# Moving the load of v of chunk 1 from GpSimd's queue to SyncE's, and that of chunk 0 from SyncE's to ScalarE's

## The chip, the cores and the metric

The kernel runs on one core of one Trainium2 chip. The metric is the device time of one execution in microseconds (us). An execution also leaves a profile: the span from the first to the last instruction is some 1.7 to 2.1 us shorter than the time. All times inside an execution are counted from the start of the span.

## The reference

Linear attention with a decay per head, in blocks, followed by a two-layer feed-forward network with an exact GELU:

```python
batch, n_heads, seq, head_dim = (4, 8, 768, 64)      # q, k, v float32; lam: one decay per head
...
intra = np.einsum('bhic,bhjc->bhij', qb, kb) * Dmask[None]
intra = np.einsum('bhij,bhjd->bhid', intra, vb)
inter = np.einsum('bhid,bhde->bhie', qb * lam_pow[None], kv_state)
out[:, :, sl] = intra + inter
...
n_tokens, d_model, d_ff = (3072, 512, 2048)
h = x @ w_in
g = 0.5 * h * (1.0 + erf(h * inv_sqrt2))
return (g @ w_out)
```

## The kernel before

The kernel cuts the attention into 24 chunks of 128 tokens (four batches, six chunks each). A prelude computes the attention of chunks 0 to 3; from then on TensorE (PE) runs the feed-forward matmuls without a break (busy for 191.12 of 191.20 us from 19.0 to 210.2 us), and the attention of later chunks is slipped in between them. Below, this second part is "the dense part"; it begins with the first `h_ps` matmul.

The loads at the start. A load by GpSimd casts float32 to bfloat16 on the way (128 KB a load on the page); v of chunk 0 alone goes by SyncE as float32 (256 KB) and is cast by ScalarE (0.61 us):

```python
def chunk_of(name, n):
    b, so = n % B, n // B
    return dram[name][b, :, so * C:(so + 1) * C, :].rearrange("h si d -> si h d")   # runs of 64 floats

def load(n, name):
    raw[n, name] = qkv_pool.tile([128, H, D], BF16, tag=name, name=f"{name}_t")
    nc.gpsimd.dma_start(raw[n, name], chunk_of(name, n))

load(0, "k")
lam_b = consts.tile([128, H], F32)
nc.sync.dma_start(lam_b, lam[None, :].to_broadcast((128, H)))
v_f = consts.tile([128, H, D], F32)
nc.sync.dma_start(v_f, chunk_of("v", 0))
# ... two iotas
for item in "q0 k1 q1 k2 q2 v1 v2 k3 q3".split():
    load(int(item[1]), item[0])
# ...
load_w_in(0, 4)          # the first of four slices of w_in
load_w_in(4, 8)
load(3, "v")
# ... two more slices of w_in, four of w_out
```

The prelude. `keep_warm(n)` issues n matmuls on zeros, which keep PE busy between pieces of real work:

```python
keep_warm(11)
# ... begin
transposes(live[0], lambda: keep_warm(1, new=False))
keep_warm(2, new=False)
scores(live[0])
late_powers()
nc.scalar.copy(live[0].v, v_f)
keep_warm(2, new=False)
transposes(live[1], lambda: keep_warm(1, new=False))
keep_warm(2)
outputs(live[0])
transposes(live[2], lambda: keep_warm(1, new=False))
nc.scalar.activation(warm, pos, ACT.Gelu)
scores(live[1])
keep_warm(1)
scores(live[2])
keep_warm(2)
outputs(live[1])
keep_warm(2)
outputs(live[2])
transposes(live[3])
keep_warm(3)
scores(live[3])
keep_warm(6)
```

In the dense part GpSimd multiplies k and q of later chunks by their decays, while DVE updates the state of a batch with two products:

```python
# GpSimd, out of first_requests()
for n in (2 * M, 2 * M + 1):
    request(n)                                   # q_hat = q * lam_p
for n in range(M, 2 * M):
    decay_k(live[n], nc.gpsimd)                  # k_dec = k * lam_m
prefetch(2 * M + 3)                              # six loads
for n in (2 * M, 2 * M + 1):
    decay_k(live[n], nc.gpsimd)
# DVE, out of next_state()
nc.vector.tensor_add(tmp, kv_ps, states[c.b])    # one input in PSUM
nc.vector.tensor_mul(new, tmp, lam_blk)          # both inputs in SBUF
```

Of the kernel before, what the change touches and what calls it, by code (L numbers as in the profile page):

```python
# [8 lines left out]
F32 = mybir.dt.float32  # L9
BF16 = mybir.dt.bfloat16  # L10
# [5 lines left out]
def kernel(  # L16
# [10 lines left out]
    nc = tc.nc  # L27

    B, H, S, D = q.shape
# [16 lines left out]
    consts = ctx.enter_context(tc.tile_pool(name="consts", bufs=1))  # L46
    w_pool = ctx.enter_context(tc.tile_pool(name="w", bufs=1))
    qkv_pool = ctx.enter_context(tc.tile_pool(name="qkv", bufs=12))
# [8 lines left out]
    raw = {}  # L57
    dram = dict(q=q, k=k, v=v)

    def chunk_of(name, n):  # L60
        b, so = n % B, n // B
        return dram[name][b, :, so * C:(so + 1) * C, :].rearrange("h si d -> si h d")
# [4 lines that stand above are left out]
# [2 lines left out]
    load(0, "k")  # L69
    lam_b = consts.tile([128, H], F32)  # L70
    nc.sync.dma_start(lam_b, lam[None, :].to_broadcast((128, H)))
    v_f = consts.tile([128, H, D], F32)
    nc.sync.dma_start(v_f, chunk_of("v", 0))

    pos = consts.tile([128, 1], F32)
    row = consts.tile([128, C], F32)
    nc.gpsimd.iota(pos, pattern=[[0, 1]], base=0, channel_multiplier=1, allow_small_or_imprecise_dtypes=True)  # L77
    nc.gpsimd.iota(row, pattern=[[1, C]], base=0, channel_multiplier=0, allow_small_or_imprecise_dtypes=True)  # L78
    for item in "q0 k1 q1 k2 q2 v1 v2 k3 q3".split():
        load(int(item[1]), item[0])  # L80

    w_in_t = w_pool.tile([128, NK1, d_ff], BF16)
# [51 lines left out]
    def late_powers():  # L134
        nc.scalar.activation(lam_c, ln_col, ACT.Exp, scale=float(C))
        nc.scalar.activation(lam_p, ln, ACT.Exp, scale=pos)
# [17 lines left out]
    live = {}  # L154

    def bank(shape, dtype, tag, name):
        return ps.tile(shape, dtype, tag=tag, name=name, bufs=4)
# [13 lines left out]
    def transposes(c, between=lambda: None):  # L171

        t_ps = [bank([128, HP, C], BF16, "m" if c.so == 0 else "sc", "t_ps") for _ in range(2)]
        for dst, src in zip(t_ps, (c.k, c.q)):
            for hp in range(HP):
                nc.tensor.transpose(dst[:, hp, :], src[:, 2 * hp:2 * hp + 2, :], ident)  # L176
            if src is c.k:
                between()
        c.kT = work_pool.tile([128, HP, C], BF16, tag="kT", name="kT")
        c.qT = work_pool.tile([128, HP, C], BF16, tag="qT", name="qT")  # L180
        nc.scalar.copy(c.kT, t_ps[0])
        nc.vector.tensor_mul(c.qT, t_ps[1], lam_q)  # L182
# [37 lines left out]
    def inter(c):  # L220
        c.o_ps = bank([128, HP, C], F32, "sc", "o_ps")
        if c.so > 0:
            for hp in range(HP):
                nc.tensor.matmul(c.o_ps[:, hp, :], states[c.b][:, hp, :], c.qT[:, hp, :],  # L224
                                 start=(hp == 0), stop=False, skip_group_check=True)

    def intra(c):
        for hp in range(HP):
            for hi in range(2):
                nc.tensor.matmul(c.o_ps[hi * D:(hi + 1) * D, hp, :], c.v[:, 2 * hp + hi, :], c.sc_m[:, hp, hi, :],  # L230
                                 start=(c.so == 0 and hp == 0), stop=True, skip_group_check=True)
        x_o = xT[c.so][:, :, c.b * C:(c.b + 1) * C]
        if c.so < 2:
            nc.scalar.copy(x_o, c.o_ps)  # L234
        else:
            nc.vector.tensor_copy(x_o, c.o_ps)  # L236

    def outputs(c):
        inter(c)
        intra(c)  # L240
# [78 lines left out]
    def keep_warm(n, new=True):  # L319

        if new:
            idle_ps[0] = bank([128, 512], F32, "m", "idle_ps")
        for _ in range(n):
            nc.tensor.matmul(idle_ps[0], idle[:, :128], idle, start=True, stop=True)  # L324
# [2 lines left out]
    nc.vector.tensor_mul(dmask, cmask[:, None, :].to_broadcast((128, H, C)),  # L327
                         lam_m[:, :, None].to_broadcast((128, H, C)))
    keep_warm(11)
    raw[0, "v"] = qkv_pool.tile([128, H, D], BF16, tag="v", name="v_t")  # L330
    for n in range(M):
        begin(n)
    transposes(live[0], lambda: keep_warm(1, new=False))
    keep_warm(2, new=False)
    scores(live[0])
    late_powers()
    nc.scalar.copy(live[0].v, v_f)
    keep_warm(2, new=False)
    transposes(live[1], lambda: keep_warm(1, new=False))
    keep_warm(2)  # L340
    outputs(live[0])
    transposes(live[2], lambda: keep_warm(1, new=False))
    nc.scalar.activation(warm, pos, ACT.Gelu)
    scores(live[1])
# [91 lines left out]
    for g in range(1, NG - 1):  # L436
        n = (g + 1) * M
# [45 lines left out]
```

## Time and profile before

| | before |
|---|---|
| time, median of the first 3 runs | 214.99 us (214.94 to 215.33) |
| span of the profiled run | 213.3 us |
| PE busy | 206.8 us, 97% |
| k of chunk 0 landed | 5.4 us |
| first transposes on PE | 5.86 us |
| first w_in slice landed | 18.91 us |
| dense part starts | 18.96 us |

A timeline line reads: start, duration, engine, source line, operation, output<-inputs, count, and in brackets the idle time before it and what ended it. The prediction shows the lines themselves.

### The profile page before, as it was taken

How to read it: one execution, taken by the hardware profiler on the slowest of the kernel's cores; microseconds unless marked ns; L12 is line 12 of the kernel's file. 1: busy time of each engine (PE TensorE's matmuls, PEld its weight loads, DVE VectorE, ACT ScalarE, POOL GpSimd, SP SyncE). 2: the span in 40 equal slices, each digit the busy share in tenths (PEclk: the TensorE clock that was granted, in tenths of full speed). 3: DMA queues.
4: the chain of work that ended last, by engine and by line, in shares of the span. 5: the costliest groups of instructions: out<-in, count | busy, mean ns of one | idle time of the engine just before them, and what ended most of it. 6: DMA issues, size and time to landing. Idle time of an engine off the chain costs nothing.

```text
span 213.3 us, 3586 instructions
## 1 busy us (share of the span) xinstructions
PE 206.8 (97%) x1474; PEld 105.3 (49%) x1474; DVE 77.8 (36%) x122; ACT 87.2 (41%) x153; POOL 103.7 (49%) x117
## 2 busy tenths in 40 slices
PE   7979999999999999999999999999999999999994
PEld 2444754556655445445445445445445445444442
DVE  4758040164395747147327047227042312000000
ACT  5653754325655221464321465321455321566121
POOL 7992433792997966929949297592000000000000
PEclk9999999999999999999999999999999999999999
DMA  8999999999999699999999989999330012100112
GB/s 87 134 160 185 206 208 187 155 213 146 151 112 116 76 124 113 233 134 65 122 110 160 199 102 129 100 168 101 123 74 0 3 49 98 52 0 0 49 49 98
DMA packets 100271, 24.48 MB, mean 115 GB/s; under 512 B 92960, under 2 KB 97312, under 8 KB 100256
## 3 DMA queue, kind: packets, MB, share of 16 engines
q0 software_dynamic: 78064, 13.51, 85.8%
q1 hardware_dynamic: 22192, 10.76, 24.6%
q8 instruction: 11, 0.18, 0.3%
q14 instruction: 4, 0.03, 0.1%
HBM read 27.27 MB, written 6.29 MB: 157 GB/s over the span
## 4 chain that ended last, share of the span: by engine, by line
PE 90%; POOL 4%; DMA 4%; issue 0%; ACT 0%; POOLq 0%
PE h_ps L263 40%; PE o_ps L275 38%; DMA w_in_t<-in_moe_w_in_dram 4%; PE o_ps L230 3%; PE sc_ps L197 3%; PE o_ps L224 2%; PE kv_ps L209 2%; POOL k_t L66 2%; PE o_ps L289 2%; POOL q_t L66 2%; PE t_ps L176 1%; POOL v_t L66 1%; ACT o_sb L293 0%; POOL row L78 0%; POOL pos L77 0%
## 5 line engine op out<-in xcount | busy, mean ns | idle before, releaser
L263 PE MATMUL h_ps<-x_t,w_in_t 128*128 128x512 bf16 (+2 forms) x432 | 86.5, 356 | 0.3 <-DMA w_in_t<-in_moe_w_in_dram 0.3
L275 PE MATMUL o_ps<-w_out_t,g_t 128*128 128x512 bf16 x368 | 82.8, 379 | 0.0
L265 ACT ACTIVATE g_t<-h_ps 128x512 bf16<-128x512 f32 (+1 forms) x99 | 57.8, 584 | 38.9 <-PE h_ps L263 38.7
L263 PEld LDWEIGHTS <-w_in_t 128*128 128x128 bf16 x432 | 39.2, 98 | 41.6 <-DMA w_in_t<-in_moe_w_in_dram 0.8
L275 PEld LDWEIGHTS <-g_t 128*128 128x128 bf16 x368 | 35.0, 98 | 41.2
L201 DVE TENSOR_TENSOR sc_m<-sc_ps,dmask 128x512 bf16<-128x512 f32 x48 | 29.9, 682 | 36.8 <-PE sc_ps L197 36.8
L280 ACT COPY o_sb<-o_ps 128x512 f32<-128x512 f32 x23 | 13.5, 586 | 69.7 <-PE o_ps L275 69.7
L189 POOL TENSOR_TENSOR q_hat<-q_t,lam_p 128x512 bf16<-128x512 bf16 x16 | 17.1, 1071 | 27.8 <-DMA q_t<-in_q_dram 12.5
L66 POOL DMA_DIRECT2D k_t<-in_k_dram x24 | 22.1, 920 | 6.4 <-DMA w_in_t<-in_moe_w_in_dram 3.8
L66 POOL DMA_DIRECT2D q_t<-in_q_dram x24 | 21.7, 903 | 3.4 <-DMA w_out_t<-in_moe_w_out_dram 3.3
L66 POOL DMA_DIRECT2D v_t<-in_v_dram x23 | 21.0, 914 | 3.4 <-DMA w_out_t<-in_moe_w_out_dram 1.7
L216 DVE TENSOR_TENSOR tmp<-kv_ps,state 128x512 f32<-128x512 f32 x16 | 11.0, 685 | 27.8 <-PE kv_ps L209 27.8
L169 POOL TENSOR_TENSOR k_dec<-k_t,lam_m 128x512 bf16<-128x512 bf16 x16 | 18.1, 1161 | 0.0
L217 DVE TENSOR_TENSOR state<-tmp,lam_blk 128x512 bf16<-128x512 f32 x16 | 13.7, 856 | 0.6
L236 DVE CAST x_t<-o_ps 128x512 bf16<-128x512 f32 x16 | 10.2, 680 | 9.4 <-PE o_ps L230 9.4
L324 PE MATMUL idle_ps<-idle 128*128 128x512 bf16 x34 | 11.7, 462 | 1.2 <-DVE idle L105 1.2
L182 DVE TENSOR_TENSOR qT<-t_ps,lam_q 128x512 bf16<-128x512 bf16 x8 | 5.5, 690 | 15.5 <-PE t_ps L176 15.4
L230 PE MATMUL o_ps<-sc_m,v_t 128*64 128x128 bf16 x192 | 8.6, 223 | 0.2
L197 PEld LDWEIGHTS <-kT 64*128 64x128 bf16 x192 | 5.7, 94 | 6.1 <-issue 3.6
L197 PE MATMUL sc_ps<-qT,kT 64*128 64x128 bf16 x192 | 8.0, 217 | 0.7 <-DVE qT L182 0.4
L230 PEld LDWEIGHTS <-v_t 128*64 128x64 bf16 x192 | 5.9, 109 | 3.2 <-issue 1.6
L234 ACT CAST x_t<-o_ps 128x512 bf16<-128x512 f32 x8 | 4.6, 585 | 5.3 <-PE o_ps L230 5.2
(41 smaller groups left out, 71.9 us busy)
## 6 DMA issues: line engine op xcount, KB each, us to landing
out_dram<-o_sb SPq DMA_DIRECT2D x23, 256.0 KB, 2.5
k_t<-in_k_dram POOLq DMA_DIRECT2D x24, 128.0 KB, 5.4
q_t<-in_q_dram POOLq DMA_DIRECT2D x24, 128.0 KB, 6.0
v_t<-in_v_dram POOLq DMA_DIRECT2D x23, 128.0 KB, 6.1
w_in_t<-in_moe_w_in_dram POOLq DMA_DIRECT2D x4, 512.0 KB, 11.1
w_out_t<-in_moe_w_out_dram POOLq DMA_DIRECT2D x4, 512.0 KB, 17.9
v_f<-in_v_dram SPq DMA_DIRECT2D x1, 256.0 KB, 3.6
kT<-k_t SPq DMA_TRANSPOSE x16, 4.0
```

What stands on the lines that cost most here:

```text
L66: nc.gpsimd.dma_start(raw[n, name], chunk_of(name, n))
L169: eng.tensor_mul(c.k_dec, c.k, lam_m[:, :, None].to_broadcast((128, H, D)))
L189: nc.gpsimd.tensor_mul(q_hat, c.q, lam_p[:, :, None].to_broadcast((128, H, D)))
L197: nc.tensor.matmul(sc_ps[hi][:, hp, :], c.kT[p, hp, :], c.qT[p, hp, :], start=True, stop=True)
L201: nc.vector.tensor_mul(c.sc_m[:, :, hi, :], sc_ps[hi], dmask_r[:, :, hi, :])
L217: nc.vector.tensor_mul(new, tmp, lam_blk)
L230: nc.tensor.matmul(c.o_ps[hi * D:(hi + 1) * D, hp, :], c.v[:, 2 * hp + hi, :], c.sc_m[:, hp, hi, :], start=(c.so == 0 and hp == 0), stop=T ...
L263: nc.tensor.matmul(h_ps[:, f, :], w, x_t[:, ki, lo:hi], start=(ki == 0 and f == 0), stop=(ki == NK1 - 1), skip_group_check=True)
L265: nc.scalar.activation(g_t[:, kf:kf + n_kf, lo:hi], h_ps, ACT.Gelu)
L275: nc.tensor.matmul(om[io], g_t[:, kf, io * C:(io + 1) * C], w_out_t[:, kf, :], start=(kf == 0), stop=(kf == NK2 - 1))
L280: nc.scalar.copy(o_sb, om[io])
L324: nc.tensor.matmul(idle_ps[0], idle[:, :128], idle, start=True, stop=True)
```

## The change

The intent: GpSimd issues its loads one after another (most take 0.88 to 0.95 us), and the first w_in slice stands behind ten of them. Taking v of chunk 1 out of that row should bring the weights in earlier. In exchange ScalarE casts one more tile.

```diff
-    v_f = consts.tile([128, H, D], F32)
-    nc.sync.dma_start(v_f, chunk_of("v", 0))
+    v_f = consts.tile([128, 2, H, D], F32)
+    nc.scalar.dma_start(v_f[:, 0], chunk_of("v", 0))
+    nc.sync.dma_start(v_f[:, 1], chunk_of("v", 1))
 ...
-    for item in "q0 k1 q1 k2 q2 v1 v2 k3 q3".split():
+    for item in "q0 k1 q1 k2 q2 v2 k3 q3".split():
 ...
-    nc.scalar.copy(live[0].v, v_f)
+    nc.scalar.copy(live[0].v, v_f[:, 0])
 ...
     outputs(live[0])
+    nc.scalar.copy(live[1].v, v_f[:, 1])
     transposes(live[2], lambda: keep_warm(1, new=False))
```

More of the change, by code (lines that the diff above doesn't have):

```diff
@@ L329 @@
     keep_warm(11)
-    raw[0, "v"] = qkv_pool.tile([128, H, D], BF16, tag="v", name="v_t")
+    for n in range(2):
+        raw[n, "v"] = qkv_pool.tile([128, H, D], BF16, tag="v", name="v_t")
     for n in range(M):
```

## The prediction

The forecast is 214.8 us: 214.99 less 0.33, the mean of its two cases (0 and -0.67 us), plus 0.1 for the maximum of two landings. The 0.27 us by which the software queue falls back rested on the author's estimate, from 290 left-over packets at 1085 per us. The 0.1 and the two halves are guesses.

> **What bounds the kernel now.** I read the page first: engine shares and the chain that ended last.
>
> ```profile
> span 213.3 us, 3586 instructions
> PE 206.8 (97%) x1474; PEld 105.3 (49%) x1474; DVE 77.8 (36%) x122; ACT 87.2 (41%) x153; POOL 103.7 (49%) x117
> PE 90%; POOL 4%; DMA 4%; issue 0%; ACT 0%; POOLq 0%
> ```
>
> TensorE is busy for 97% of the span, and 90% of the last chain is its work. Next, the table of stretches, which splits the span where I expected the regimes to change. Columns: stretch, its length, then busy time and instruction count of PE, PEld, DVE, ACT and POOL, the granted clock, the DMA share, GB/s.
>
> ```profile
> 10.50:11.70 1.20, 0.20 (x3) 0.09 (x3) 0.00 (x0) 1.18 (x3) 1.20 (x3) 1.00 2.29 146
> 11.70:18.70 7.00, 6.55 (x66) 3.13 (x66) 5.16 (x9) 2.64 (x5) 4.97 (x7) 1.00 1.46 173
> 19.00:210.20 191.20, 191.12 (x1352) 98.02 (x1352) 66.27 (x102) 76.62 (x133) 88.17 (x93) 1.00 1.08 113
> ```
>
> From 19.0 to 210.2 us PE is busy for 191.12 of 191.20 us at full clock. The change alters none of that work, so the end moves only as far as the first matmul of the dense part (h_ps) moves. That starts at 18.96 us. What sets it? The chain in order of time, early pieces:
>
> ```profile
> 1.26 1.06 POOL k_t L66
> ...
> 7.09 1.75 POOL v_t L66 x2
> 8.84 0.87 POOL k_t L66
> 9.71 0.79 POOL q_t L66
> 10.50 8.41 DMA w_in_t<-in_moe_w_in_dram
> 18.91 0.05 issue
> 18.96 4.07 PE h_ps L263 x24
> ```
>
> By this chain, GpSimd issues ten chunk loads one after another and then the first w_in slice, which lands 8.41 us later. This is what the change attacks. But the chain shows only the last releaser, so I read PE's own timeline for the second latest:
>
> ```profile
> 10.23 0.38 PE L324 MATMUL idle_ps<-idle 128*128 128x512 bf16 x1
> 11.61 0.40 PE L176 MATMUL t_ps<-ident,q_t 128*128 128x128 bf16 x4 [1.00 <-DMA q_t<-in_q_dram]
> ...
> 16.90 0.40 PE L197 MATMUL sc_ps<-qT,kT 64*128 64x128 bf16 x8
> 17.23 1.47 PE L324 MATMUL idle_ps<-idle 128*128 128x512 bf16 x6
> 18.96 4.07 PE L263 MATMUL h_ps<-x_t,w_in_t 128*128 128x384 bf16 x24 [0.26 <-DMA w_in_t<-in_moe_w_in_dram]
> ```
>
> PE waits for w_in only 0.26 us. Its in-order prelude ends at 18.70, and this prelude is tied to another transfer: the q of chunk 2, which lands at 11.6 and before which PE idles 1.00 us. From there to 18.70 is 7.09 us of transposes, scores, outputs and filler matmuls in a fixed order. So two branches end within 0.2 us: **branch W**, the w_in slice (18.91), and **branch Q**, q of chunk 2 plus 7.09 us (18.70).
>
> Last, the DMA view in narrow windows, packets by queue. The two lines below are for 3.5 to 4.0 us; a chunk load is 1024 packets.
>
> ```profile
> q1 hardware_dynamic: 346, 0.09, 76.7%
> q0 software_dynamic: 178, 0.02, 71.0%
> ```
>
> In 3.0 to 3.5 us the hardware queue alone moved 482; in 4.0 to 4.5 the software queue moved 546. All three are near 500 packets per half microsecond. For 5.0 to 12.5 us the view counts 8134 software packets, that is 542 per half microsecond: from about 3 us on the shared engines are full. One chunk load costs 1024 / 1085 per us = 0.94 us of them, against 0.87 us of issue on GpSimd, so service and not issue sets the pace.
>
> [...]
>
> **The change part by part.**
> - *Removed from the software queue*: v of chunk 1, 0.87 us of issue and 0.94 us of service ahead of w_in. (By my count nine loads stay ahead of the first slice; the tenth, v of chunk 3, is between slices.) It stood **behind** q of chunk 2, so branch W gains up to 0.94 us and branch Q nothing.
> - *Added to the hardware queues*: another 1024 packets early. In before, v of chunk 0 is issued at 1.20 us, sends its first packets near 2.3 and is done by about 4.2. In after, ScalarE can issue v of chunk 0 at 0.7, half a microsecond earlier, with SyncE's load beside it. From the half-microsecond counts I estimate some 900 packets by 3.0 us (v0 run forward half a microsecond about 680, v1 about 220), 500 more by 3.5 and 350 by 4.0, which leaves some 300 of 2048. [...] The software queue falls back by about 290 / 1085 = 0.27 us, and as it is full from there on, it keeps the delay.
> - *Branch W*: -0.94 + 0.27 = -0.67, so 18.24 us.
> - *Branch Q*: +0.27 from the same delay. Against it: lags from issue to landing for k0, q0, k1, q1, k2, q2 are 4.1, 3.7, 4.2, 4.2, 4.2, 5.4 us. Only the last is out of line, and between 9.0 and 9.5 us the packet count dips to 426. If that was a chance stall, q2 would land at 6.18 + 4.2 + 0.27 = 10.65 next time and branch Q would end at 17.74; if it is systematic, at 18.97. I give each half.
> - *ScalarE*: one issue (0.4 us, taken from SyncE's rows) lies before 2.43 us, where ScalarE waits for lam until 3.61: free. The second cast (0.61 us, as the v_t<-v_f row) goes after x_t of chunk 0 at 10.68 us. It pushes kT of chunk 2 from 11.18 to about 11.8, needed at 12.79, and the Gelu table load's end from 12.47 to 13.1, with ScalarE's next work at 14.40: free.
> - *Sum*: start of h_ps is the later branch. Systematic: max(18.24, 18.97) = 18.97, no gain. Chance: max(18.24 + 0.05, 17.74) = 18.29, a gain of 0.67. The mean is -0.33; the maximum of two jittering landings costs some 0.1, so about -0.2 us from 214.99, which is 214.8.
>
> **Rivals.** *Full gain*: the hardware loads are through before GpSimd's first packets (3.4 us), nothing is delayed, W gains 0.94 and Q lands early: 214.0 to 214.1. For it: engines idle until 2.3 us. Against: the first q1 packets come slowly, about 200 per half microsecond before 3.0, and 2048 packets at 500 per half microsecond need 2 us. *Branch Q takes the place of W*: v traffic delays k0 and q2 by more than I think [...], say 0.5 to 0.7, and the prelude with its six filler matmuls ends at 19.2 to 19.4: 215.3 to 215.4. For it: only 0.26 us separates the branches. Against: PE has 1.00 us of idle ahead of q2, so delays of k0 alone are absorbed. *ScalarE becomes the bound*: the cast delays kT of chunk 2 and outputs of chunk 1. It would need over 1 us more than I count; up to +0.3 us. *A late lam*: its 128 tiny packets now compete with v; ln, lam_m, dmask and qT slip by a few tenths, again ahead of the 1.00 us of idle: nothing.
>
> **Range and chances.** Best case -0.9, worst +0.5, both unlikely: 214.2 to 215.4 holds 8 in 10. 2% is 4.3 us. The whole prelude is 19 us and neither branch can move by that; a build whose dense part runs otherwise is all I leave: faster 0.01, same 0.98, slower 0.01.
>
> **What would show it.** The first h_ps start should move from 18.96 to 18.3 to 19.0 and the dense part keep 191.2 us. The w_in slice should be issued near 9.63 instead of 10.50 and land near 18.2. k of chunk 0 should land 0.2 to 0.3 us later than 5.4. If branch Q binds, h_ps shows no wait for w_in and follows the six filler matmuls at once. I am wrong if the dense part changes length, if k of chunk 0 doesn't slip, or if ScalarE shows up as releaser in the prelude.

## The result, and the profile after

The changed kernel took 217.04 us (median of 5 fast runs, 216.72 to 218.15), the kernel before in the same rounds 214.96 us (214.74 to 215.33). A ratio here is the mean time of one kernel's fast runs over that of the other's of the same rounds, so not quite the ratio of the medians: 1.0107, 95% interval 1.0078 to 1.0136. The change made the kernel about 1% slower. By the 2% rule this is "same", and the predicted range (214.2 to 215.4) did not hold it.

From the page of the changed kernel: the span, the engines, the granted PE clock in 40 slices (in tenths of full speed) and the chain that ended last.

```profile
span 215.1 us, 3562 instructions
PE 206.2 (96%) x1449; PEld 106.0 (49%) x1474; DVE 75.8 (35%) x122; ACT 87.8 (41%) x154; POOL 102.7 (48%) x116
...
PEclk9889999999999999999999999999999999999999
...
PE 89%; DVE 5%; DMA 3%; issue 1%; POOL 1%; ACT 0%; POOLq 0%; DVEq 0%
```

New are the two 8s in the clock row, the second and third slices, and DVE with 5% of the chain. (PE shows 25 fewer matmuls, but the weight loads are 1474 as before: some matmul records are missing.)

PE's timeline of the changed kernel, the lines that answer to those of before:

```profile
1.19 4.69 PE L325 MATMUL idle_ps<-idle 128*128 128x512 bf16 x11 [1.19 <-DVE idle L106]
7.47 0.40 PE L177 MATMUL t_ps<-ident,k_t 128*128 128x128 bf16 x4 [1.58 <-DMA k_t<-in_k_dram]
...
13.66 0.39 PE L177 MATMUL t_ps<-ident,q_t 128*128 128x128 bf16 x4
...
19.26 1.47 PE L325 MATMUL idle_ps<-idle 128*128 128x512 bf16 x6
20.57 4.06 PE L264 MATMUL h_ps<-x_t,w_in_t 128*128 128x384 bf16 x24
```

The dense part starts at 20.57 us instead of 18.96. It no longer waits for w_in: the slice was issued at 9.62 and landed 6.8 us later, at 16.4 us, 2.5 us earlier than before, and lay unused for 4 us. Nor does PE wait for q of chunk 2 at 13.66. What is late is the very first input: k of chunk 0 landed 6.2 us after its issue at 1.25, so at 7.45 us instead of 5.4, and PE idled for 1.58 us ahead of it.

The table of stretches for two windows of 3.41 us in the changed kernel. Columns: stretch, length, busy time and count of PE, PEld, DVE, ACT and POOL, granted clock, DMA share, GB/s. The bounds are the moments at which the trace's clock record changes.

```profile
5.58:8.99 3.41, 1.55 (x13) 0.62 (x11) 1.35 (x2) 2.56 (x9) 3.41 (x5) 1.00 2.43 155
8.99:12.40 3.41, 3.06 (x21) 1.86 (x21) 1.86 (x3) 0.88 (x2) 3.41 (x5) 0.50 3.23 150
```

After a window in which PE worked for only 1.55 us of 3.41, its clock was halved for the next 3.41 us. This falls on the scores of chunk 0 and the transposes of chunk 1.

The clock record of this trace begins at 5.58 us. Before that PE ran at half pace as well: the matmuls on zeros (512 columns) come 427 ns apart there and 216 ns apart later. The first fillers are slow in every trace here: 11 of them took 4.01 to 4.88 us, 7 took 3.17 (e7), 15 took 4.79 to 6.33 (e6, e10, e12, e13) and 20 took 7.39 (e1), where 11 at 216 ns would take some 2.6. The records begin between 4.01 us (e6) and 8.54 us (e7); e8's trace has none. The clock row and the mean clock of a run leave this start out, so "clock 1.000" below means whole from the beginning of the record on.

So three things had to be explained: why k came 2 us late, how much of the loss is the clock, and whether the dense part itself changed. Counted from its start to the end of the span it is 194.6 us long (215.13 - 20.57) against 194.3 before (213.26 - 18.96).

### The profile page after: what moved, and what is told of

It reads as the page before. It is cut to its first block, busy times and chain, and to the rows that moved or that the text cites. A ratio compares the mean times of both kernels' runs of the same rounds, so it can differ in the third digit from the quotient of the medians.

```text
span 215.1 us, 3562 instructions
## 1 busy us (share of the span) xinstructions
PE 206.2 (96%) x1449; PEld 106.0 (49%) x1474; DVE 75.8 (35%) x122; ACT 87.8 (41%) x154; POOL 102.7 (48%) x116
## 4 chain that ended last, share of the span: by engine, by line
PE 89%; DVE 5%; DMA 3%; issue 1%; POOL 1%; ACT 0%; POOLq 0%; DVEq 0%
PE h_ps L264 37%; PE o_ps L276 37%; PE o_ps L231 3%; PE sc_ps L198 3%; DMA q_t<-in_q_dram 3%; PE t_ps L177 2%; PE o_ps L225 2%; PE kv_ps L210 2%; PE o_ps L290 2%; PE idle_ps L325 2%; DVE state L218 1%; DVE tmp L217 1%; DVE sc_m L202 1%; DVE qT L183 1%; POOL k_t L66 0%
## 5 line engine op out<-in xcount | busy, mean ns | idle before, releaser
L276 PE MATMUL o_ps<-w_out_t,g_t 128*128 128x512 bf16 x356 | 81.3, 379 | 1.2 <-issue 0.8
L190 POOL TENSOR_TENSOR q_hat<-q_t,lam_p 128x512 bf16<-128x512 bf16 x16 | 17.9, 1120 | 26.7 <-issue 13.3
L66 POOL DMA_DIRECT2D v_t<-in_v_dram x22 | 20.0, 909 | 4.2 <-DMA w_in_t<-in_moe_w_in_dram 2.4
L170 POOL TENSOR_TENSOR k_dec<-k_t,lam_m 128x512 bf16<-128x512 bf16 x16 | 17.1, 1092 | 0.0
L218 DVE TENSOR_TENSOR state<-tmp,lam_blk 128x512 bf16<-128x512 f32 x16 | 12.1, 754 | 0.6
L182 ACT COPY kT<-t_ps 128x512 bf16<-128x512 bf16 x8 | 4.7, 589 | 6.8 <-PE t_ps L177 6.8
```

Source lines behind the costliest of these rows:

```text
L170: eng.tensor_mul(c.k_dec, c.k, lam_m[:, :, None].to_broadcast((128, H, D)))
L190: nc.gpsimd.tensor_mul(q_hat, c.q, lam_p[:, :, None].to_broadcast((128, H, D)))
L276: nc.tensor.matmul(om[io], g_t[:, kf, io * C:(io + 1) * C], w_out_t[:, kf, :], start=(kf == 0), stop=(kf == NK2 - 1))
```

## The experiments

Theories, as they came up after the result:
- **L**: the two early float32 loads delay k of chunk 0, and this delay passes through the prelude.
- **C**: most of the loss is the half clock, which the gap on PE ahead of k brings about.
- **G**: since GpSimd has one load fewer, its k_dec and q_hat products come earlier in the dense part and fall on DVE's state products, which then last longer and hold PE up. (This came up with the second group of runs.)

All kernels gave correct results but e3. Each run lists time and mean granted clock; 0.992 is what one 3.41 us window at half clock makes of a span of 213 us (0.5 x 3.41 / 213 = 0.008). A run over 1.5% above the fastest of its kernel is classed as slow.

### First group: what is the gap worth, and what delays k?

**e1_more_fillers.**

```diff
-    keep_warm(11)
+    keep_warm(20)
```

> The changed kernel with 20 instead of 11 filler matmuls ahead of the first transposes, so that PE has work until about 7.6 us, when k of chunk 0 has landed (7.46 us in the changed kernel, 5.44 before). Theory C (the loss is the half clock of 8.76 to 12.17 us, itself a result of the 1.58 us gap on PE): clock 1.000 throughout, k of chunk 0 as late as in the changed kernel, the dense part starts near 19.0 to 19.4 instead of 20.57, time 215.0 to 215.8. Rival L (the loss is the late landing of k alone, pushed through the whole prelude): the clock may be whole, but the dense part still starts at 20.3 to 20.6 and the time stays at 216.7 to 217.2.

Measured: clock 1.000 in 4 of 4 runs; 215.39, 215.47, 216.80 and 218.76 us; ratio of the fast runs 1.0066 (1.003 to 1.0102); before 214.42. k came as late as in the changed kernel, but the whole clock brought the dense part to 19.77 us (the 20 fillers overran k: transposes at 8.42). That speaks for C against L alone, though the start and one of the three fast runs (216.80) lie above what C expected. (By the clock record the half window of the changed kernel is 8.99 to 12.40 us, not 8.76 to 12.17.) The 218.76 us run, classed as slow, was the profiled one, and its dense part was 197.1 us long (216.83 - 19.77). The chain of the last releasers of that run, inside the dense part:

```profile
62.63 2.40 DVE state L218
65.03 0.61 DVE tmp L217
65.64 0.02 issue
65.66 3.81 DVE state L218
69.47 2.41 DVE sc_m L202 x4
```

Here DVE and not PE sets the pace: two state products take 2.40 and 3.81 us. In the kernel before the corresponding ones take 0.81 us. GpSimd's k_dec and q_hat ran from 62.37 to 68.92 us in this run. That is where theory G came from; as one slow run is no evidence, it had to be looked for in fast ones.

**e2_one_queue.**

```diff
-    nc.scalar.dma_start(v_f[:, 0], chunk_of("v", 0))
+    nc.sync.dma_start(v_f[:, 0], chunk_of("v", 0))
```

> Both float32 loads of v on the queue of SyncE, none on that of ScalarE. If the loads delay GpSimd's first load by their number (each 1024-packet load starts about 0.9 us after the one before it), k of chunk 0 lands as late as in the changed kernel, 7.2 to 7.7 us, and the time is 216.5 to 217.3. If a second hardware queue is what hurts, the first software packet comes near 3.5 us again, k lands near 5.4 to 6.2 and the time is 214.8 to 215.6.

Measured: k landed at 1.25 + 5.8 = 7.05 us, nearly as late as with two queues, so the second hardware queue isn't the main cause (0.4 of the 2.05 us went with it). The times were 214.90, 216.18, 216.75 and 218.21 us with clocks of 1.000, 0.992, 0.990 and 1.000, the last one slow; ratio 1.0069 (1.0026 to 1.0111). The profiled run was the one of 214.90 us: the same late k, a gap of 1.22 us, the clock whole, and the dense part at 18.94 us. The two fast runs of this kernel with a half window took over 1 us more than the one without; that is one run against two.

**e3_long_packets** (wrong result).

```diff
-    nc.scalar.dma_start(v_f[:, 0], chunk_of("v", 0))
-    nc.sync.dma_start(v_f[:, 1], chunk_of("v", 1))
+    # 128 rows of 2 KB that lie together, instead of 1024 runs of 256 B
+    nc.scalar.dma_start(v_f[:, 0].rearrange("p h d -> p (h d)"), long_rows(0))
+    nc.sync.dma_start(v_f[:, 1].rearrange("p h d -> p (h d)"), long_rows(1))
```

> Wrong result on purpose: the same two loads of 256 KB on the same two queues, but as 128 rows of 2 KB that lie together in memory, so 128 packets each where there were 1024. If the number of packets (descriptors) delays k of chunk 0, k lands at 5.0 to 5.8 us, PE has no gap, clock 1.000, time 214.3 to 215.3. If the bytes do, k stays at 7 us or later and the time at 216.7 to 217.2.

Measured: k landed at 6.05 us: of the 2.05 us of delay, 1.4 went with the packets and 0.65 stayed with the bytes or the loads as such. Neither expectation was met in full. The first packet of k came no earlier (4.55 us; 4.27 in the changed kernel); the gain came after it, with 436 software packets from 4.5 to 5.0 us against 114. Times 214.49, 214.88, 217.09 and 218.51 us (the last slow, with clock 0.992); ratio 1.0047 (0.9987 to 1.0108), inconclusive as a time.

**e4_v1_later.**

```diff
-    nc.scalar.dma_start(v_f[:, 0], chunk_of("v", 0))
-    nc.sync.dma_start(v_f[:, 1], chunk_of("v", 1))
+    nc.sync.dma_start(v_f[:, 0], chunk_of("v", 0))
 ...
         nc.scalar.activation(lam_q[:, hp, :], row, ACT.Exp, scale=ln_col[:, hp:hp + 1])
+    nc.scalar.dma_start(v_f[:, 1], chunk_of("v", 1))
```

> v of chunk 0 alone on SyncE's queue as in the kernel before; v of chunk 1 on ScalarE's queue, issued only after the lam_q powers (near 5.3 to 6.6 us). k of chunk 0 should land near 5.4 again and the clock stay at 1.000. If early contention and the clock are the whole loss: time 214.5 to 215.3, with w_in landing near 18.9 since the packets only move. If the software queue loses what this load takes in mid-prelude, q of chunk 2 lands up to 0.9 later than 11.6 and the dense part starts at 19.3 to 19.9: time 215.3 to 215.9.

Measured: 214.97, 215.37, 215.39 and 217.46 us; ratio 1.0062 (1.0013 to 1.0112). k landed near 5.5 us again and PE started on it at 5.86; the clock was 1.000 in three runs and 0.998 in one. PE could start on q of chunk 2 only at 12.36 us (before: 11.61), and the dense part started at 19.29. The load of v had only moved its 1024 packets into the middle of the prelude, where the software loads then came later (PE waited 0.68, 0.54 and 0.56 us for three of them), as the second expectation had it. (w_in landed at 17.0 us, not near 18.9.)

### Second group: taking the two suspected losses away

**e5_pool_block_later** and **e6_both_undone.** The scratch loads are never read; they only put GpSimd's products back in time.

```diff
         prefetch(2 * M + 3)
+        for i in range(2):
+            scratch = consts.tile([128, H, D], BF16, name=f"scratch{i}")
+            nc.gpsimd.dma_start(scratch, chunk_of("v", 1))
         for n in (2 * M, 2 * M + 1):
             decay_k(live[n], nc.gpsimd)
```

```diff
 # e6: as e5, and
-    keep_warm(11)
+    keep_warm(15)
```

> The changed kernel with two scratch loads (never read) issued by GpSimd just ahead of the k_dec of chunks 8 and 9, which puts that block of GpSimd's products (62.3 us in the changed kernel, 63.75 before) back by about 1.8 us. Theory G (besides the clock, the dense part is at times held up by DVE's state products, which grow from 0.69 us to between 1.3 and 3.8 us when GpSimd's k_dec and q_hat fall on them, and the missing load made them fall earlier): the clock is still at 0.992 in most runs, the runs of 217.5 and more are gone, time 216.2 to 216.9, no state product of chunks 4 to 7 longer than 1.4 us. If G is wrong, the spread of the changed kernel (216.7 to 218.2) stays.

> The changed kernel with both suspected losses taken away: 15 filler matmuls ahead of the first transposes instead of 11, and the two scratch loads of the run before. If the clock (C) and the collision of DVE with GpSimd (G) are together the whole loss, clock 1.000 and time 214.3 to 215.3, so within 0.5 us of the kernel before, with k of chunk 0 still 2 us late. If a late k costs by itself, 216 or more.

Measured, e5: five runs with clocks of 0.990 to 0.992 at 216.53, 216.54, 216.54, 216.64 and 217.18 us, and one with the whole clock at 215.33 us. The runs with the half clock took 216.54 - 215.33 = 1.2 us more in one and the same kernel. Not all of this lies in the prelude: the profiled run of 216.54, set beside e6's of 215.33, starts the dense part 0.78 us later (20.01 against 19.23), and its dense part is 0.42 us longer (194.62 against 194.20). Ratio 1.0095 (1.0066 to 1.0124). The runs of 217.5 and more are gone, as expected, but one run (217.18) is above 216.9, and the longest state product of chunks 4 to 7 took 1.41 us, just over the 1.4 expected. It started at 64.40, beside the k_dec that the scratch loads had put back to 64.13: with a prelude this late they don't keep the two apart.

Measured, e6: six runs between 215.33 and 215.44 us, clock 1.000 (one 0.998); before 214.52 in the same rounds; ratio 1.0045 (1.0027 to 1.0063). This is less than half of the loss, and the spread is gone. It missed its upper bound by 0.06 us, and with 215.36 - 214.52 = 0.84 us it isn't within 0.5 us of the kernel before: a late k costs something by itself. In e6 PE idled for 1.43 us ahead of k, and the clock stayed. The stretch, columns as above:

```profile
4.01:7.42 3.41, 1.98 (x10) 0.70 (x9) 1.60 (x3) 2.96 (x7) 3.41 (x5) 1.00 2.04 196
```

PE worked for 1.98 of 3.41 us here. In e2's profiled run it was 1.78 (5.52 to 8.93), and the clock stayed as well. It fell after windows with 1.55 (the changed kernel), 1.30 (e11), 1.16 (e5), 1.50 and 1.38 us (e9, 9.49 and 64.10 us on), and stayed after one with 1.68 (e15, 15.67 us on). In the traces of before and of the changed kernel PE worked for 2.29 us (before, 9.44 to 12.86) or more in every other window up to the end of the matmuls, and the clock stayed. So in these traces it isn't the gap as such that goes with the half clock, but how little PE worked within one window of 3.41 us: 1.55 us and less against 1.68 and more. Where the windows lie differs from run to run (one edge is at 5.58, 4.64, 4.20, 4.01 us in these traces), so one kernel can have runs of both kinds.

**e7_before_with_a_gap.**

```diff
 # on the kernel before
-    keep_warm(11)
+    keep_warm(7)
```

> The kernel before with 7 instead of 11 filler matmuls, so that PE idles some 1.5 us ahead of the first transposes, with all loads as before. Theory C: the clock falls to half for 3.4 us in part of the runs or all (0.992), and the time rises to 215.5 to 217 although no transfer changed. Rival (the clock of the changed kernel fell for another reason than the gap): clock 1.000, time 214.3 to 215.

Measured: clocks of 0.990 to 0.991 in three of six runs (never under 0.997 in the kernel before), so the gap alone does it with no transfer changed. But the times were 214.41 to 215.22, median 214.93 against 214.52, ratio 1.0022 (1.0002 to 1.0041), and runs with the low clock were no slower than the others (214.82, 214.93 and 215.22 against 214.41, 214.94 and 214.94). The first half of the expectation held, the second missed. The six means don't sort the runs into with and without, though: in the profiled one (214.41, mean 1.000) the record begins only at 8.54 us, and until then the transposes and scores of chunk 0 ran slow (four transpose matmuls took 0.61 to 0.63 us, 0.39 later). That trace still shows where the loss goes: PE doesn't wait for q of chunk 2, waits 0.34 us for w_in, and starts the dense part at 18.35. Whatever the slower matmuls cost, w_in came later. So the low clock cost little in this kernel (medians 214.93 with it, 214.94 without), where PE ended up waiting for a transfer; that this wait is the reason is likely, not shown.

**e8_w_in_first.**

```diff
 # on the kernel before
-    for item in "q0 k1 q1 k2 q2 v1 v2 k3 q3".split():
+    for item in "q0 k1 q1 k2 q2 v1 v2".split():
 ...
     load_w_in(0, 4)
+    load(3, "k")
+    load(3, "q")
     load_w_in(4, 8)
 ...  # transposes(3), scores(3) and outputs(3) as visits of the dense part at its matmul blocks 2, 4, 7
```

> An attempt to beat both, on the kernel before: GpSimd loads the first w_in slice ahead of k and q of chunk 3, and the transposes and scores of chunk 3 move from the prelude into the dense part. If the prelude's end is set by the transfers ahead of w_in and by q of chunk 2 as read, the slice lands near 17.0 instead of 18.9, the dense part starts there and grows by about 0.8 us (16 transposes and scores): 213.6 to 214.2. If a later transfer or DVE stalls the dense part instead: 214.5 to 215.5.

Measured: 214.68 us (214.37 to 216.30), before 214.52; ratio 1.0023 (0.9994 to 1.0051). The dense part started at 16.50 us, but PE then waited 0.87 us for the second slice, which had been pushed back, and had the chunk's own work added. By the first `kv_ps` at 26.14 us it was level with e7, whose dense part began at 18.35 us (`kv_ps` at 25.91). An attempt that failed: behind the first slice the next one waits.

### Third group: the four corners, and where the early w_in slice went

**e11_changed_again** and **e12_fillers_only** complete a table of two by two with e5 and e6.

```diff
 # e11: no edit.   e12:
-    keep_warm(11)
+    keep_warm(15)
```

> The changed kernel, unaltered, beside the other runs on one chip, for a second trace and the spread. Expected: 216.5 to 218.2, clock 0.992 or 0.998 in nearly all runs, k of chunk 0 landed near 7.4 us.

> The changed kernel with 15 instead of 11 early fillers and nothing else: the fourth corner beside the changed kernel (neither), e5 (scratch loads only) and e6 (both). Theory C and G add up: clock 1.000 in nearly all runs; the best runs at 215.3 as in e6, but a spread up to 217 from the collisions of DVE and GpSimd. If G has no part, the runs are as tight as in e6 (215.3 to 215.5).

| | as changed | with scratch loads (GpSimd's products later) |
|---|---|---|
| 11 fillers | e11: 215.31, 216.84, 216.93, 216.94, 217.59, 217.66 | e5: 215.33, 216.53, 216.54, 216.54, 216.64, 217.18 |
| 15 fillers | e12: 215.34, 215.35, 215.38, 216.74, 218.72, 219.37, 219.41 | e6: 215.33, 215.34, 215.34, 215.39, 215.41, 215.44 |

e11 repeated the result: ratio 1.0108 (1.0075 to 1.014). In e12 the clock was 0.992 in two runs (219.37 and 219.41) and 0.998 to 1.000 in five, and with the whole clock the fast runs still spread over 1.4 us, where e6 has 0.1: that is what theory G expects without C. (The ratio of e12's fast runs is 1.0037, 1.0013 to 1.006; it leaves out the three runs from 218.72 us up, which are classed as slow, so what follows rests on the fast ones: 215.34 to 216.74.) Its profiled run, 216.74 us, starts the dense part at 19.29 us, e6 at 19.23; the rest is 195.5 us in e12 (214.84 - 19.29) and 194.2 in e6 (213.43 - 19.23). DVE's state products of chunks 4 to 7 in e12 and GpSimd's products beside them:

```profile
58.90 1.57 DVE L218 TENSOR_TENSOR state<-tmp,lam_blk 128x512 bf16<-128x512 f32 x1
61.11 0.81 DVE L218 TENSOR_TENSOR state<-tmp,lam_blk 128x512 bf16<-128x512 f32 x1
62.56 1.41 DVE L218 TENSOR_TENSOR state<-tmp,lam_blk 128x512 bf16<-128x512 f32 x1
64.61 0.81 DVE L218 TENSOR_TENSOR state<-tmp,lam_blk 128x512 bf16<-128x512 f32 x1
```

```profile
62.31 2.56 POOL L170 TENSOR_TENSOR k_dec<-k_t,lam_m 128x512 bf16<-128x512 bf16 x2
64.83 2.48 POOL L190 TENSOR_TENSOR q_hat<-q_t,lam_p 128x512 bf16<-128x512 bf16 x2
```

And in e6:

```profile
58.84 0.69 DVE L218 TENSOR_TENSOR state<-tmp,lam_blk 128x512 bf16<-128x512 f32 x1
60.16 0.69 DVE L218 TENSOR_TENSOR state<-tmp,lam_blk 128x512 bf16<-128x512 f32 x1
61.49 0.83 DVE L218 TENSOR_TENSOR state<-tmp,lam_blk 128x512 bf16<-128x512 f32 x1
62.96 0.81 DVE L218 TENSOR_TENSOR state<-tmp,lam_blk 128x512 bf16<-128x512 f32 x1
...
64.15 2.11 POOL L170 TENSOR_TENSOR k_dec<-k_t,lam_m 128x512 bf16<-128x512 bf16 x2
```

In e12 the third state product starts at 62.56, just after GpSimd's k_dec at 62.31, and both last longer (1.41 us against 0.83 in e6, the two k_dec 2.56 against 2.11). In e6 GpSimd begins when DVE is done with its fourth (63.77). In the kernel before, GpSimd begins at 63.75, and DVE is done at 63.49: it had been spared by a quarter of a microsecond. PE loses its time in one place, a wait of 1.1 us for DVE ahead of the scores at 64.62. In e11's profiled run (216.84, dense part 194.7) the third and fourth state product took 1.42 and 1.82 us beside k_dec.

Not all is covered. The four products of e12 took 4.60 us, those of e6 3.02. Of these 1.58 us the first product has 0.88, and it fell beside GpSimd's issuing of loads, not its products. Up to there GpSimd does the same in both kernels, so the scratch loads can't have removed that part; what lengthens it stays open.

**e9_no_early_v.**

```diff
 # both float32 loads taken from the start and put behind the lam_q powers:
+    nc.scalar.dma_start(v_f[:, 0], chunk_of("v", 0))
+    nc.scalar.dma_start(v_f[:, 1], chunk_of("v", 1))
```

> The changed kernel with both float32 loads of v issued by ScalarE only after the lam_q powers, so that no hardware load runs ahead of GpSimd's first one. Asked: what does one early float32 load cost the first software load? The first software packet came at 3.44 us with one early load (before) and at 4.27 with two (changed). If each load puts it back by some 0.8 us, it comes at 2.4 to 2.8 here and k of chunk 0 lands at 4.4 to 4.8. If one load was free and only the second hurt [...], it comes at 3.3 to 3.5 again and k lands at 5.3 to 5.5. The time says little, since v of chunk 0 comes late: 215 to 217.

Measured (one look): the first software packet at 3.01 us, k landed at 1.25 + 3.6 = 4.85 us, time 221.04 us. Both lie between the two expectations: the first load costs 0.4 us of packet start, the second 0.8. The time lies above the announced 215 to 217, with two half windows (mean clock 0.984); as v of chunk 0 comes late here, it says nothing about the question.

**e10_less_filler.**

```diff
 # on e6
-    keep_warm(6)
+    keep_warm(2)
 ...
-    nc.scalar.copy(live[1].v, v_f[:, 1])
     transposes(live[2], lambda: keep_warm(1, new=False))
+    nc.scalar.copy(live[1].v, v_f[:, 1])
```

> Run e6 (15 fillers, scratch loads) with the last six filler matmuls cut to two and the cast of v of chunk 1 placed after kT of chunk 2. Where did the earlier w_in slice go? Theory: it landed at 18.2 to 18.5 in the changed kernel as the prediction had it, but the prelude, which starts 1.6 us later and has no waits left to give up, ends after it. Then cutting about 0.9 us of filler and up to 0.3 of waiting moves the start of the dense part from 19.2 to 18.2 to 18.5 and the time to 214.3 to 214.8, level with the kernel before. If the start stays near 19.2, something else than the prelude's length sets it.

Measured: the dense part started at 18.35 us, the time was 214.74 us (214.46 to 215.14) against 214.67, ratio 1.0009 (0.999 to 1.0028): level with the kernel before, as expected. w_in had landed at 16.3 us, not at 18.2 to 18.5 as the expectation had it, so 2 us of it were still unused. (One of the eleven runs of before in this group took 1203 us; it isn't among the fast runs.)

### Fourth group: what was still open

**e14_half_of_v1_early.**

```diff
-    nc.sync.dma_start(v_f[:, 1], chunk_of("v", 1))
+    nc.sync.dma_start(v_f[:, 1, :4], chunk_of("v", 1)[:, :4])
 ...  # behind the lam_q powers:
+    nc.scalar.dma_start(v_f[:, 1, 4:], chunk_of("v", 1)[:, 4:])
```

> The changed kernel with only four of the eight heads of v of chunk 1 loaded early by SyncE (512 packets); the other four by ScalarE after the lam_q powers. Landing of k of chunk 0 by early float32 packets so far: none 4.9 us, 1024 5.4, 2048 7.45 (in 256 packets of 2 KB: 6.05). If the second load costs by its number of packets, k lands half way, 6.2 to 6.6. If the start of one more load is what costs, 7.2 to 7.5. If half of it still fits into idle engines, 5.4 to 5.7.

Measured (one look): k landed at 6.35 us, half way, as the number of packets would have it; PE idled for 0.30 us ahead of it, clock 1.000, dense part at 18.36, time 214.43 us. With none, 1024, 1536 and 2048 early float32 packets, k lands at 4.85, 5.4, 6.35 and 7.45 us: the second thousand costs 2 us, the first only about half of one.

**e13_shorter_prelude** and **e15_before_shorter_prelude.** The same edit, on the changed kernel (with 15 fillers and the later cast of v) and on the kernel before:

```diff
     outputs(live[1])
-    keep_warm(2)
+    transposes(live[3])
+    keep_warm(1)
     outputs(live[2])
-    transposes(live[3])
-    keep_warm(3)
     scores(live[3])
-    keep_warm(6)
```

> The changed kernel with 15 early fillers, the cast of v of chunk 1 after kT of chunk 2, and a shorter end of the prelude: the transposes of chunk 3 ahead of the outputs of chunk 2, three of the seven small groups of fillers there dropped. In the changed kernel the first w_in slice lands at 16.4 us and nothing uses it before 20.6 (18.35 in e10). If the prelude's own length is what hides it, the dense part starts near 16.8 to 17.1, PE waits at most 0.8 for the second slice (19.0 to 20.2), and the time is 213.2 to 214.0, below the kernel before (214.5). If the later slices bind instead, as in e8: 214.3 to 214.8.

> The kernel before with the same shorter end of the prelude and nothing else: is it the change that gains in e13, or the order alone? If w_in binds in the kernel before as its chain said (landing 18.9 in its trace, 18.0 to 18.9 over its runs), the dense part starts at 18.0 to 18.9 however short the prelude is, with a wait for w_in of 0.5 us and more, and the time stays at 213.9 to 214.7. If it drops below 213.9, the order alone gains.

Measured, e13: 213.52, 213.79, 213.82, 213.84, 213.86 and 215.16 us, clock 1.000 in all; before 214.53 (213.88 to 215.27). Five of the six are below the fastest of eleven runs of the kernel before; the ratio of all fast runs is 0.9979, 95% interval 0.9954 to 1.0005, so it just isn't settled by that measure. PE's timeline of e13 at the point in question:

```profile
16.50 0.40 PE L198 MATMUL sc_ps<-qT,kT 64*128 64x128 bf16 x8 [0.21 <-DVE qT L183]
16.96 2.76 PE L264 MATMUL h_ps<-x_t,w_in_t 128*128 128x384 bf16 x16
20.34 1.47 PE L264 MATMUL h_ps<-x_t,w_in_t 128*128 128x384 bf16 x8 [0.62 <-DMA w_in_t<-in_moe_w_in_dram]
```

The dense part starts at 16.96 us, 2.0 us earlier than before, without a wait for w_in; of this 0.62 us goes to the second slice.

Measured, e15: 214.28 and 214.60 us in the two runs with the whole clock, 216.16 to 218.73 in four with 0.984 to 0.992; ratio 1.0055 (1.0013 to 1.0098), which leaves two slow runs out. In its profiled run the slice lands at 17.7 us and PE waits for it:

```profile
17.80 2.77 PE L263 MATMUL h_ps<-x_t,w_in_t 128*128 128x384 bf16 x16 [1.56 <-DMA w_in_t<-in_moe_w_in_dram]
```

So the order alone gains nothing. That the longer wait is what costs four of the six runs their clock is likely but not shown: the profiled run kept its clock. The change does bring weights in early; only a prelude that is short enough can use them.

## Why the prediction was wrong

**What bounds the kernel: right.** The start of the dense part moved by 1.61 us and is the bulk of the loss. "The change alters none of that work" was right of PE's work but left out GpSimd: one load fewer moves its later products too (k_dec from 63.75 to 62.33 us).

**Branch W: right in direction, mis-sized.** The slice was issued at 9.62 as foretold and landed at 16.4, not 18.24. The gain in this pair of traces was 2.5, not 0.67: the lag from issue to landing fell from 8.4 to 6.8 us. Part of this is scatter. In the ten traces with this order of GpSimd's loads and both float32 loads early (the changed kernel, e1 to e3, e5, e6, e10 to e13) the lag was 6.5 to 7.7 us, mean 6.95, and 7.7 in e11, the same kernel; with the loads of the kernel before (its own trace, e7 and e15) it was 8.4, 7.8 and 7.2, mean 7.8. By the means the gain is some 1.7 us, the 0.88 of the earlier issue included. Why the lag falls is not settled.

**The step that failed: "Added to the hardware queues".** It put the fall-back of the software queue at 0.27 us. Measured: 2.05 us. The estimate ran v of chunk 0 forward by half a microsecond because ScalarE issues it at 0.7; it was issued at 0.74, but its first packet came at 2.35 us (before, by SyncE: 2.27), that of v of chunk 1 at 3.25 and the first of k at 4.27 (before: 3.44). The estimate had 1750 float32 packets done by 4.0 us; the trace has 733, fewer than the 1006 of the kernel before, which had one such load. The rest then met the first software packets. The DMA view of the changed kernel for 4.0 to 4.5 us (queue, packets, MB, share of engine time; q10 is ScalarE's queue):

```profile
q10 hardware_dynamic: 356, 0.09, 79.9%
q1 hardware_dynamic: 176, 0.04, 39.2%
q0 software_dynamic: 26, 0.00, 10.4%
```

In the kernel before, the software queue had this in the same half microsecond:

```profile
q0 software_dynamic: 546, 0.07, 217.5%
```

558 packets in half a microsecond are the full engines of the prediction, but the software queue gets 26 of them, where before it had 546. By e2 (7.05 us with one queue), e3 (6.05 with 256 long packets) and e14 (6.35 with 1536) the delay goes mostly with the number of packets ahead of k, not with the second queue. Of the 2.05 us, 0.83 is the later first packet (4.27 against 3.44), and the rest follows it; long packets took away only from the rest (e3). Why the software queue gets only 26 of the 558 stays open; whether it had more work by then, no run shows.

**The rival that was called absorbed.** The second rival named the right mechanism (v traffic delays k0, the prelude ends later) and argued against it with 1.00 us of idle. The idle is real in the profiled run: counted from k's transposes to the dense part, a prelude at full clock without later waits for data takes 11.8 us (e6: 7.41 to 19.23; e12: 7.46 to 19.29), and in the kernel before it took 13.10 us, of which 1.26 were the waits for q and w_in. A delay of 1.61 us on PE (5.86 to 7.47) exceeds this by some 0.35; e12's start, 19.29 against 18.96, has 0.33. But the traces speak for a chance stall, one of the two halves that branch Q was given: q of chunk 2 took 5.4 us to land there and 4.4, 4.4 and 4.7 us in e7, e8 and e15, whose loads are the same up to it. With 4.4 us it lands at 10.6, when PE is ready for it, and the 1.00 us isn't there to absorb anything. The prediction counted on this idle against the rival and at the same time gave its absence one half.

**What no part of it saw.** First the clock: 20.57 - 19.29 = 1.28 us of the start, where the half window is 8.99 to 12.40 us. Where it lies earlier it costs less: 0.98 in e11 (20.27 - 19.29), 0.78 in e5 against e6. The late k alone and the half clock make up the whole 0.33 + 1.28 = 1.61. Second, DVE's state products: 0.3 us in the profiled run (194.6 - 194.3) and 1.3 us in e12's, a fast run, against e6 (195.5 - 194.2). In the changed kernel's own trace PE falls back by 0.35 us at the scores at 64.92, and the one long product ahead of them is this:

```profile
60.18 1.31 DVE L218 TENSOR_TENSOR state<-tmp,lam_blk 128x512 bf16<-128x512 f32 x1
```

It fell beside loads; GpSimd's k_dec began only at 62.33. So the 0.3 us of that run isn't the collision that theory G describes. That the time of GpSimd's products matters is shown by e12 against e6, and e11's trace has the collision; how much of the slower runs it explains is not shown. About 0.2 us of the difference in time lies outside the span.

**Against the medians** the split is a little different: e6, with clock and collision gone, is 0.84 us slower than its kernel before. The half clock adds 0.8 to 1.3 us, so it is about half of the loss, not most of it as theory C had it. The kernel before was profiled in one of its slower runs (span 213.3; others 212.0 to 213.5), so the late k costs between 0.3 and 0.8 us.

**The small terms: right but for one.** ScalarE's issue and its earlier part cost nothing. The second cast did delay kT of chunk 2 until PE waited for it 0.27 us in most traces, where the prediction had a margin of 1 us, so ScalarE does show up as releaser in the prelude, one of its own signs of being wrong. A late lam (ln at 4.06 instead of 3.61) cost nothing.

## What to carry to other kernels

A transfer that "only uses idle engines" early on can still stand ahead of the one input that everything waits for (k landed at 7.45 us here, at 5.4 before): check what lands first, not only what lands last. Work out what a delay does to idle time on PE, since the gap of 1.6 us here, with most of it in one clock window, cost another 0.8 to 1.3 us after it. And where a load is taken from an engine that also computes, its later work moves too (k_dec by 1.4 us here): look at what that will meet. A gain that is hidden behind a second, nearly equal branch shows only when both are shortened, as in e13.

## What the runs show of the clock, the queues and DVE

- The half clock: for the next 3.41 us the clock was halved after windows of 3.41 us in which PE was busy for 1.16 (e5), 1.30 (e11), 1.38 and 1.50 (e9) and 1.55 us (the changed kernel); it stayed whole after 1.68 (e15), 1.78 (e2) and 1.98 us (e6).
- The first software load behind hardware loads: k landed at 4.85 (e9), 5.4 (before), 6.35 (e14) and 7.45 us (the changed kernel) behind 0, 1024, 1536 and 2048 packets of 256 B. From 4.0 to 4.5 us the queues of ScalarE, SyncE and GpSimd moved 356, 176 and 26 packets in the changed kernel.
- DVE's state product beside GpSimd: it took 0.69 us at its shortest. Beside k_dec or q_hat it took up to 2.15 us in a fast run (e10, at 68.60) and 3.81 in the slow run of e1, but only 0.82 and 0.81 in the changed kernel (63.45 and 64.90). The sum ahead of it (`tmp`) stayed at 0.68 to 0.69 in the same stretches. Beside the issuing of loads alone it took 1.57 us in e12 (58.90) and 1.31 in the changed kernel (60.18), but 0.69 and 0.81 in the kernel before (59.91 and 61.23). No run tested this by itself.
